# Channel attention and two gated layers: block 0 goes through the softmax itself, and the softmax is folded into w_in beside it

## The chip, the core and the metric

The kernel runs on one core of a Trainium2 chip. The metric is the time of one execution on the device, in microseconds (us). The kernel before took 1212.53 us (median of three runs, 1211.35 to 1214.38). The profile shown here was taken in a further execution of 1211.48 us.

## The reference

There are 6016 tokens of 256 channels. q, k, v and all weights come as 64-bit floating point numbers or 32-bit ones; the kernel computes in 32 bits.

```
qn = q / (norm over tokens of q + 1e-6);  kn likewise
a  = softmax(kn^T qn / tau)          # 256 x 256, over the last axis
x  = v @ a                           # 6016 x 256
h  = x @ w_in                        # 6016 x 2048
P  = a0 + a1 h + a2 h^2 + a3 h^3;    Q = 1 + |b0||h| + |b1| h^2
y  = (P / (Q + 1e-6)) @ w_out        # 6016 x 256
g  = sigmoid(y @ w_gate);  u = y @ w_val          # 6016 x 1536 each
out = (g * u) @ w_out2
```

## The kernel before, in words

**Two arithmetics.** A matmul of 32-bit floats (`f32`) takes four passes of the systolic array. Most of the kernel splits each operand instead into a rounded high part and the rest (`hi`, `lo`, type `fp32r`) and adds three one-pass products. A split costs a copy (on ACT or DVE) and a subtraction (on DVE or POOL).

**Stage 1, scores and norms.** q and k lie interleaved in `kqk` and are loaded in 15 chunks of one, two or four tiles of 128 tokens (`LOADS`). For each tile TensorE adds k^T q into `s_ps` (L488, f32): 256 columns for chunks marked `s` in `KG`, 384 for chunks marked `g`, whose extra columns give the squared norms of k on the diagonal. ACT squares each chunk (L509), DVE or POOL add some of the squares up (L518, `UNIT` says which), and TensorE sums them over the tokens (L457: all-ones weights by 256 columns, L461: squares as weights by one column of ones) into `nrm`. So the norms of q stand along the free axis, the same in all partitions, and those of k one to a partition.

**Loads.** All big loads go through SyncE's queue in the order of the string `ORDER` (`x` a chunk of `kqk`, `n` the tokens of v of block 0, `i`, `o`, `g`, `v`, `2` chunks of w_in, w_out, w_gate, w_val and w_out2, 1 MB each as 64-bit numbers). A chunk of `kqk` is put into the room of a weight that is loaded later. a, b and tau are loaded from ACT's queue at the start.

**Weights.** Each of the 17 weight chunks is turned into 32-bit floats: ACT scales the upper words (L679), ACT or DVE shifts the lower ones (L682 or L686, the string `TOP`), DVE joins the two (L690). Then it is split: high part on ACT or DVE (L807 or L811, `HI`), rest on DVE or POOL (L814, `LOW`).

**Softmax.** From `nrm` and the diagonals come 1/norm (L574 to L588; for q with DVE operations on 256 columns), then the scaled scores and their row maximum (L600), the exponentials with row sums (L608), the row sums' reciprocals (L621), the transposes of the exponentials (L615) and their copy to SBUF (`et_sb`, L625). `WARM` matmuls without a use (L632) may run while TensorE has nothing else.

**Fold.** v @ a @ w_in is computed as v @ (a @ w_in): each of the four chunks of w_in (512 columns) is multiplied by the transposed exponentials (L739, f32), and the evacuation from PSUM multiplies by the reciprocal row sums: L753/L756 for chunk 0, which is kept whole and split later by L774/L778, and L759/L761 for chunks 1 to 3, which are split at once.

**Blocks.** The tokens are then worked in 12 blocks, block 0 of 384 tokens and the rest of 512. A block's first layer has 8 steps: h of 256 columns of w_in (L899 in f32 for the two steps of block 0 that use chunk 0; L884/L886/L888 as three products otherwise, for which v is split by L849/L852), three ACT passes over h (L908 to L912), the rational function on DVE, ACT and POOL (L914 to L936; the reciprocal is a seed with an arctangent correction), and the sum into y (L946 in f32 for block 0, L964 to L974 later). The second layer of a block (L1010 to L1047) runs between the first-layer steps of the next.

**Order.** Every operation is given an engine, a cost and a due time; a planner in the kernel lays them out by these, and each engine's instructions are then issued in that order. The dictionaries `VT`, `VT0`, `VT1`, `WT` hold the due times and the strings above the choices of engine and buffer. An engine works its list strictly in order: an instruction that waits holds up all behind it.

Of the kernel before, what the change touches and what calls it, by code (L numbers as in the profile page):

```python
# [9 lines left out]
F32 = mybir.dt.float32  # L10
# [29 lines left out]
VT1 = {'h': -17955.3, 'u': 1533.3, 'ab': -991.9, 'sq': -3411.4, 'v': -162.2, 'w': 1751.0, 'Q': -2494.2, 'seed': 18354.6, 't': -325.8, 'at': -3730.8, 'y': 617.1, 'g': 2768.2, 'hi': 2217.8, 'lo': -1222.6, 'yh': 2990.1, 'yl': 344.8, 'G': 4863.1, 'sig': -6142.7, 'sv': -15292.6, 'hi2': 3414.6, 'lo2': 2277.0, 'oh': -11134.2, 'ol': -140.4, 'base': 851.8, 'ev': 2619.7}  # L40

VT0 = {'h': -1990.9, 'u': 14971.4, 'ab': -134.3, 'sq': 11037.5, 'v': 4305.9, 'w': -9165.5, 'Q': -4668.5, 'seed': 15588.7, 't': -6249.8, 'at': -10702.8, 'y': -4704.4, 'g': -1165.7, 'hi': 757.1, 'lo': -493.3, 'yh': 4573.9, 'yl': -5536.7}

WT = {'ci': -142.1, 'ci_d': -17724.1, 'co': 1739.6, 'co_d': 5275.5, 'cg': 1385.4, 'cg_d': 1785.4, 'cv': -1917.9, 'cv_d': -1783.3, 'c2': -4767.0, 'c2_d': 2905.7, 'wp': -3829.7, 'wp_d': 241.4, 'b0': 7059.9, 'b1': -3149.2, 'b2': -3.8, 'm0': -8935.8, 'm1': 3.6, 'e0': -6822.5, 'cvl': 2835.9, 'alt': 5000.0, 'wpp': 4734.9, 'v0': -3576.2, 'ri': -4427.7, 'ri_d': 11199.1, 'ro': 12944.7, 'ro_d': -9707.8, 'cvm': 4036.8}


ORDER = 'xxxxxxxinxxgogxxxxov2x2ix2oiogivv'
# [18 lines left out]
WARM = 8  # L66
# [46 lines left out]
class Plan:  # L113
# [40 lines left out]
    def schedule(self):  # L154
# [67 lines left out]
        while len(order) < len(self.ops):  # L222
# [54 lines left out]
def tile_channel_attention_two_moes(  # L277
# [78 lines left out]
    class Weight:  # L356
# [36 lines left out]
        def keys(self, col):  # L393
            return [(self.key(col), p, h) for p in range(2) for h in range(2)]
# [52 lines left out]
    def sum_mm(sq, n, q_only):  # L447
        first_sum["n"] = first_sum.get("n", 0) + 1

        def run():  # L450
            first_sum["n"] -= 1
            late = not first_sum["n"]
            w = C if q_only else 2 * C
            v_ = sq.ap().rearrange("p a c -> p (a c)")
            for i in range(n):
                q0 = i * w + (0 if q_only else P)
                mm(out=nrm.ap()[:, 0:C], lhsT=ones, rhs=v_[:, q0:q0 + C], start=0 not in first_sum,  # L457
                   stop=late and i == n - 1 and q_only)
                first_sum[0] = True
                for h in () if q_only else (0, 1):  # L460
                    mm(out=nrm.ap()[:, C + h:C + h + 1], lhsT=v_[:, i * w + 3 * P * h:i * w + 3 * P * h + P],  # L461
                       rhs=ones[:, 0:1], start=False, stop=late and i == n - 1 and h == 1)
        return run
# [30 lines left out]
    for k, (c, i, n) in enumerate(units):  # L494
# [18 lines left out]
        elif direct:  # L513
            pl.op(PE, n * (.433 if g else .893), t_s + (c + .7) * SUM_AT, sum_mm(sq, n, g), [sq, "ones"], [nrm], tail=0.01)
# [13 lines left out]
    for k, (x, lo_, n) in enumerate(((a, 0, 4), (b, 4, 2), (tau, 6, 1))):  # L528
        pl.op(ACT, .1, -30000.0 + k, lambda x=x, lo_=lo_, n=n: nc.scalar.dma_start(
            out=sm[:, lo_:lo_ + n], in_=bcast(x, n)), (), ["sm_" + "abt"[k]], tail=2.4)  # L530

    def coefs():
        V = nc.vector
        V.tensor_scalar(out=cf[:, 0:4], in0=sm[:, 0:4], scalar1=KAPPA, scalar2=None, op0=ALU.mult)
# [4 lines left out]
        V.tensor_scalar(out=cf[:, 6:7], in0=cf[:, 6:7], scalar1=4.0, scalar2=None, op0=ALU.mult)  # L539

# [9 lines left out]
    pl.op(DVE, 0.6, -29000.0, coefs, ["sm_a", "sm_b", "sm_t"], ["cf", "sm_c"], port=True)  # L550
# [5 lines left out]
    rn = pl.buf("w", [P, 3, C], at=t_n)  # L556

    def diag_k():
        for h in range(2):
            nc.vector.scalar_tensor_tensor(  # L560
                out=rn.ap()[:, 2, :P], in0=s_ps.ap()[:, h, h * C:h * C + P], scalar=1.0, in1=ident, op0=ALU.mult,
                op1=ALU.mult, accum_out=sm[:, 22 + h:23 + h])

    def nrm_add():
        nc.vector.tensor_tensor(out=sm[:, 22:24], in0=sm[:, 22:24], in1=nrm.ap()[:, C:C + 2], op=ALU.add)

    if any(kg):
# [6 lines left out]
    pl.op(ACT, c_act(C, 1, 1), tn, lambda: nc.scalar.activation(  # L574
        out=rn.ap()[:, 1, :], in_=nrm.ap()[:, 0:C], func=ACTF.Sqrt, bias=sm[:, 8:9]), [nrm, "sm_tiny"], [(rn, 1)])
    pl.op(ACT, .2, tn, lambda: nc.scalar.activation(
        out=cf[:, 14:16], in_=x2(), func=ACTF.Sqrt, bias=sm[:, 8:9]), [xk, "sm_tiny"], ["sm_n"])

    def twice_norm(x, root, y):
        V = nc.vector  # L580
        V.reciprocal(out=y, in_=root)
        V.tensor_tensor(out=y, in0=x, in1=y, op=ALU.mult)
# [539 lines left out]
```

## Time and profile before

| | |
|---|---|
| median of three runs | 1212.53 us |
| the profiled execution | 1211.48 us |
| its span, first to last instruction | 1209.4 us |
| TensorE (PE) busy | 1177.8 us, 97% |
| VectorE (DVE) busy | 974.2 us, 81% |
| ScalarE (ACT) busy | 834.6 us, 69% |
| GpSimd (POOL) busy | 521.2 us, 43% |
| data moved | 43.30 MB |

The shares are means over stages of different kinds. The span is best cut at about 62 us (norms complete), 81 us (first useful matmul after the softmax) and 150 us (all weights ready, blocks overlap). The profile's "granted clock" is the share of full speed that TensorE got in a stretch. A matmul of f32 leaves two rows in the trace, so a count of 16 stands for 8 matmuls.

### The profile page before, as it was taken

The page shows a single profiled execution, that of the slowest core. Times are in us where ns is not written, and L with a number is a line of the kernel's source. Part 1 is how long each engine was busy: PE and PEld are TensorE (multiplying, and loading weights), DVE is VectorE, ACT ScalarE, POOL GpSimd, SP SyncE. Part 2 cuts the span into 40 slices and gives each one's busy share as a digit, 9 for nine tenths or more (in the row PEclk, how much of TensorE's full clock was granted, in tenths as well). Part 3 has the DMA queues.
Part 4 walks back from the last instruction along what each step waited for, and adds up shares of the span by engine and source line. Part 5 has one row for each costly group of instructions (what it writes and reads, how often), then busy time and mean ns, then how long its engine had stood idle before and what let it go on. Part 6 is the DMA issues. An engine that isn't in the chain of part 4 may idle for free.

```text
span 1209.4 us, 13151 instructions
## 1 busy us (share of the span) xinstructions
PE 1177.8 (97%) x5160; PEld 963.6 (80%) x5160; DVE 974.2 (81%) x838; ACT 834.6 (69%) x983; POOL 521.2 (43%) x266
## 2 busy tenths in 40 slices
PE   7968999999999999999999999999999999999998
PEld 5845699788888888888888888888888888888877
DVE  2799988798788789788789789789888878878911
ACT  5778877676677677677677577677677677667622
POOL 5523255355354345345345345345345435435422
PEclk9979999999999999999999999999999999999999
DMA  9960000000100100100100100100000000000000
GB/s 361 400 251 18 18 1 1 31 1 1 36 1 1 35 1 1 35 1 1 35 1 1 35 1 1 36 1 1 29 7 1 18 18 1 18 1 1 18 1 17
DMA packets 15613, 43.30 MB, mean 36 GB/s; under 512 B 1344, under 2 KB 1856, under 8 KB 14272
## 3 DMA queue, kind: packets, MB, share of 16 engines
q1 hardware_dynamic: 14976, 42.21, 9.3%
q8 instruction: 40, 0.66, 0.2%
q10 hardware_dynamic: 576, 0.27, 0.1%
q14 instruction: 21, 0.17, 0.0%
HBM read 36.31 MB, written 6.16 MB: 35 GB/s over the span
## 4 chain that ended last, share of the span: by engine, by line
PE 87%; DVE 5%; DMA 4%; ACT 2%; issue 1%; POOL 0%; SPq 0%; DVEq 0%
PE pO L1039 10%; PE pH L884 6%; PE pH L886 6%; PE pH L888 6%; PE pY L974 6%; PE pY L966 6%; PE pY L964 6%; PE pG L1010 5%; PE pV L1010 5%; PE pG L1012 5%; PE pO L1047 5%; PE pV L1012 5%; PE pG L1014 5%; PE pV L1014 5%; DMA win<-in_kqk_dram 2%; DMA wo<-in_moe_w_out_dram 1%
## 5 line engine op out<-in xcount | busy, mean ns | idle before, releaser
L1032 POOL TENSOR_TENSOR lo<-sig,hi 128x512 fp32r<-128x512 f32 (+1 forms) x143 | 248.8, 1745 | 337.6 <-ACT hi L1028 337.6
L956 POOL TENSOR_TENSOR lo<-w,hi 128x1024 fp32r<-128x1024 f32 x88 | 217.1, 2467 | 265.3 <-ACT hi L951 218.4
L933 DVE SCALAR_TENSOR_TENSOR a<-a,s 128x1024 f32<-128x1024 f32 (+1 forms) x94 | 167.6, 1784 | 54.1 <-ACT a L930 54.1
L910 ACT ACTIVATE a<-pH,cf 128x1024 f32<-128x1024 f32 (+1 forms) x92 | 101.7, 1105 | 100.0 <-PE pH L888 100.0
L1039 PE MATMUL pO<-hi,wo 128*128 128x512 f32 (+1 forms) x580 | 151.6, 383 | 0.0
L920 DVE SCALAR_TENSOR_TENSOR a<-a,s 128x1024 f32<-128x1024 f32 (+1 forms) x94 | 113.6, 1209 | 46.7 <-ACT s L912 44.9
L884 PE MATMUL pH<-vhi,win 128*128 128x512 f32 (+1 forms) x364 | 141.8, 390 | 2.6 <-DVE w L917 2.6
L936 DVE SCALAR_TENSOR_TENSOR w<-w,cf,a 128x1024 f32<-128x1024 f32 (+1 forms) x95 | 140.2, 1476 | 2.9
L888 PE MATMUL pH<-vhi,win 128*128 128x512 f32 (+1 forms) x364 | 141.3, 388 | 0.0
L886 PE MATMUL pH<-vlo,win 128*128 128x512 f32 (+1 forms) x364 | 141.3, 388 | 0.0
L930 ACT ACTIVATE a<-a 128x1024 f32<-128x1024 f32 (+1 forms) x96 | 99.9, 1041 | 58.2 <-DVE a L928 56.3
L1025 DVE TENSOR_TENSOR sig<-sig,pV 128x512 f32<-128x512 f32 (+2 forms) x145 | 96.6, 667 | 53.0 <-PE pV L1014 51.9
L928 DVE TENSOR_TENSOR a<-a,s 128x1024 f32<-128x1024 f32 (+1 forms) x89 | 138.2, 1553 | 0.0
L964 PE MATMUL pY<-hi,wo 128*128 128x512 f32 x352 | 137.1, 390 | 0.0
L966 PE MATMUL pY<-hi,wo 128*128 128x512 f32 x352 | 137.1, 389 | 0.0
L1028 ACT ACTIVATE hi<-sig 128x512 fp32r<-128x512 f32 (+2 forms) x145 | 90.5, 625 | 58.0 <-DVE sig L1025 57.6
L1039 PEld LDWEIGHTS pO<-hi,wo 128*128 128x128 f32 x580 | 108.1, 188 | 21.0
L917 DVE SCALAR_TENSOR_TENSOR w<-w,cf,pH 128x1024 f32<-128x1024 f32 (+1 forms) x92 | 116.4, 1265 | 1.7
L1010 PE MATMUL pG<-yhi,wg 128*128 128x512 f32 (+1 forms) x288 | 112.2, 389 | 1.6 <-ACT yhi L985 1.1
L1023 ACT ACTIVATE sig<-pG 128x512 f32<-128x512 f32 (+2 forms) x145 | 85.3, 589 | 39.8 <-PE pG L1014 24.2
L1012 PE MATMUL pG<-ylo,wg 128*128 128x512 f32 (+1 forms) x288 | 111.0, 385 | 0.8 <-DVE ylo L987 0.8
L1010 PE MATMUL pV<-yhi,wv 128*128 128x512 f32 (+1 forms) x288 | 110.9, 385 | 0.0
(231 smaller groups left out, 2322.4 us busy)
## 6 DMA issues: line engine op xcount, KB each, us to landing
wo<-in_moe_w_out_dram SPq DMA_DIRECT2D x7, 1024.0 KB, 15.9
wo<-in_kqk_dram SPq DMA_DIRECT2D x6, 1024.0 KB, 13.6
v<-in_v_dram SPq DMA_DIRECT2D x11, 512.0 KB, 3.6
out_dram<-v SPq DMA_DIRECT2D x10, 512.0 KB, 2.8
win<-in_moe_w_in_dram SPq DMA_DIRECT2D x4, 1024.0 KB, 15.2
wg<-in_moe_w_gate_dram SPq DMA_DIRECT2D x3, 1024.0 KB, 19.0
wv<-in_moe_w_val_dram SPq DMA_DIRECT2D x3, 1024.0 KB, 16.5
win<-in_kqk_dram SPq DMA_DIRECT2D x2, 1024.0 KB, 16.5
```

What stands on the lines that cost most here:

```text
L884: mm(out=hp.ap()[:, i, :n], lhsT=WIN.at(f * P, 0, z), rhs=vhi.ap()[:, z, :n], start=(z == 0), stop=False)
L886: mm(out=hp.ap()[:, i, :n], lhsT=WIN.at(f * P, 0, z), rhs=vlo.ap()[:, z, :n], start=False, stop=False)
L888: mm(out=hp.ap()[:, i, :n], lhsT=WIN.at(f * P, 1, z), rhs=vhi.ap()[:, z, :n], start=False, stop=(z == 1))
L933: pl.op(DVE, c_dve(N), vt + vp['y'] * d, lambda: stt(out=V(y_), in0=V(a_), scalar=ATAN_C, in1=V(s_), op0=ALU.add, op1=ALU.mult), [a_] + S_ ...
L936: pl.op(DVE, c_dve(N, 1), vt + vp['g'] * d, lambda: stt(out=V(w_), in0=V(w_), scalar=col(A0), in1=V(y_), op0=ALU.add, op1=ALU.mult), [w_, ...
L956: lambda: e_lo.tensor_tensor(out=V(lo), in0=V(w_), in1=V(hi).bitcast(F32), op=ALU.subtract),
L964: mm(out=y_ps.ap()[:, z, :n], lhsT=WO.at(f * C, 0)[:, sl], rhs=hi.ap()[:, i, :n], start=(f == 0), stop=False)
L966: mm(out=y_ps.ap()[:, z, :n], lhsT=WO.at(f * C, 1)[:, sl], rhs=hi.ap()[:, i, :n], start=False, stop=False)
L1010: mm(out=gp[i].ap()[:, :n], lhsT=wt.at(f * P, 0, z), rhs=yhi.ap()[:, z, :n], start=(z == 0), stop=False)
L1012: mm(out=gp[i].ap()[:, :n], lhsT=wt.at(f * P, 0, z), rhs=ylo.ap()[:, z, :n], start=False, stop=False)
L1032: lambda sg=sg, hi=hi, lo=lo, sl=sl, e=e: e.tensor_tensor(out=lo.ap()[:, sl], in0=sg.ap()[:, sl], in1=hi.ap()[:, sl].bitcast(F32), op=ALU. ...
L1039: mm(out=o_ps.ap()[:, z, sl], lhsT=WO2.at(f * C, i)[:, z * P:(z + 1) * P], rhs=hi.ap()[:, sl], start=(f == 0 and i == 0), stop=False)
```

## The change

- **Block 0.** The exponentials are divided by their row sums in place (`over`, on DVE, per half). v of block 0 is multiplied by them on TensorE (`x_mm`, four f32 matmuls of 384 columns), ACT copies the result to SBUF (`x0`), and all eight steps of block 0 multiply x0 by w_in as it is (f32, `h_plain`). v of block 0 is no longer split.
- **Fold.** The transposes and the fold of w_in come with later due times, for use from block 1 on. Every half chunk of 256 columns is folded by itself into the PSUM tile pG or pV, and goes from there to its split parts at once: high part on ACT, rest on DVE. L753 to L778 go.
- **Norms.** The squares of q too are summed with the squares as weights and one column of ones: four columns of `nrm` in place of 258. 1/norm is four DVE operations on 128 x 4; those of q are put on a diagonal (`diag_q`), spread over the partitions by two matmuls with all-ones weights, and copied to SBUF.
- **Small loads.** a, b and tau go through SyncE's queue, b and tau after the fifth load, a after the 25th.
- **Replanned.** ORDER, KG, UNIT, PLC (which room a chunk of `kqk` takes), TOP, HI, LOW, the buffers, and all due times of blocks 0 and 1 and of the weights are new; those of the later blocks are not. WARM is 6 in place of 8.

```diff
-ORDER = 'xxxxxxxinxxgogxxxxov2x2ix2oiogivv'
+ORDER = 'xx2xvxxxgxvxxxxxgxxoxoiioiongvi22'
-KG = 'ssgsssssssssgss'
+KG = 'ggssssssssssgsg'
-TOP = 'aaaddaaaaadddddda'
-HI = 'dadaaaddaddad'
-LOW = 'ddddpppppddpp'
-T_PS = '...YYHHYYY.Y2YYHY'
+TOP = 'adaaaaaddaaddadad'
+HI = 'dadadaadddaaa'
+LOW = 'pdppdpdpppppp'
+T_PS = 'HYYYH..HYY.YYYY..'
-S0 = 'gssssssg'
-T0 = 'pppppdpd'
+S0 = 'sssgsgsg'
+T0 = 'pdpdpppd'
...
-                mm(out=nrm.ap()[:, 0:C], lhsT=ones, rhs=v_[:, q0:q0 + C], start=0 not in first_sum,
-                   stop=late and i == n - 1 and q_only)
...
+                for m, c0 in ((0, 0), (1, P)) if q_only else ((2, 0), (0, P), (1, 2 * P), (3, 3 * P)):
+                    mm(out=nrm.ap()[:, m:m + 1], lhsT=v_[:, i * w + c0:i * w + c0 + P], rhs=ones[:, 0:1],
...
+        def over(h=h):
+            r = sm[:, 18 + h:19 + h]
+            nc.vector.tensor_scalar(out=r, in0=sm[:, 16 + h:17 + h], scalar1=1e-9, scalar2=None, op0=ALU.add)
+            nc.vector.reciprocal(out=r, in_=r)
+            nc.vector.tensor_scalar(out=e_sb.ap()[:, h, :], in0=e_sb.ap()[:, h, :], scalar1=r, scalar2=None,
+                                    op0=ALU.mult)
...
+            for z in range(2):
+                mm(out=x_ps.ap()[:, z, :n0], lhsT=e_sb.ap()[:, h, z * P:(z + 1) * P], rhs=nat0.ap()[:, h, :n0],
+                   start=h == 0, stop=h == 1)
...
+            pl.op(ACT, c_act(2 * m, 1), pv, lambda part=part, both_=both_: nc.scalar.activation(
+                out=part(0), in_=both_(), func=ACTF.Copy), [two], [(key, 0, q)])
+            pl.op(DVE, c_dve(2 * m), pv, lambda part=part, both_=both_: nc.vector.tensor_tensor(
+                out=part(1), in0=both_(), in1=part(0).bitcast(F32), op=ALU.subtract), [two, (key, 0, q)], [(key, 1, q)])
...
+            def h_plain(i=i, f=f):
+                w = win_f[f // 4][0]()
+                for z in range(2):
+                    mm(out=hp.ap()[:, i, :n], lhsT=w[:, z, f % 4 * P:f % 4 * P + P], rhs=nat.ap()[:, z, :n],
+                       start=(z == 0), stop=(z == 1))
```

## Rows read from the trace of the kernel before

**Rows 1.** The page's first part: busy time, share of the span, instructions of each engine.

```profile
PE 1177.8 (97%) x5160; PEld 963.6 (80%) x5160; DVE 974.2 (81%) x838; ACT 834.6 (69%) x983; POOL 521.2 (43%) x266
```

**Rows 2.** Windows: stretch, length, busy time of each engine, granted clock, DMA share, GB/s.

```profile
0.00:62.65 62.65, 55.08 (x238) 44.69 (x238) 31.98 (x35) 42.31 (x44) 33.44 (x22) 1.00 0.97 381
62.65:80.84 18.19, 6.81 (x22) 5.55 (x22) 17.81 (x33) 12.08 (x17) 4.72 (x2) 0.62 0.95 370
80.84:150.00 69.16, 63.23 (x235) 42.21 (x233) 66.03 (x73) 56.98 (x71) 19.20 (x12) 1.00 0.05 16
150.00:1204.00 1054.00, 1051.75 (x4664) 870.43 (x4663) 857.72 (x699) 722.66 (x851) 463.84 (x231) 1.00 0.03 11
50.00:139.60 89.60, 71.51 (x275) 50.04 (x274) 86.62 (x107) 70.65 (x89) 28.22 (x16) 0.92 0.38 142
```

**Rows 3.** Timeline of PE in stage 1: start, length, instruction, count, idle before.

```profile
14.05 5.32 PE L488 MATMUL pO<-wo 128*128 128x384 f32 x16
33.02 7.07 PE L488 MATMUL pO<-wo 128*128 128x256 f32 x32
53.57 1.13 PE L488 MATMUL pO<-wv 128*128 128x256 f32 x4 [1.39 <-DMA wv<-in_kqk_dram]
55.33 0.68 PE L457 MATMUL gv<-w,ones 128*128 128x256 f32 x2
56.21 1.97 PE L457 MATMUL gv<-w,ones 128*128 128x256 f32 x8
```

**Rows 4.** Timeline of all engines from 62 to 81 us, norms to fold.

```profile
62.63 2.36 POOL L814 TENSOR_TENSOR wo<-s,wo 128x1024 fp32r<-128x1024 f32 x1 [3.98 <-DVE wo L811]
63.77 2.30 DVE L690 SCALAR_TENSOR_TENSOR lo<-lo,win 128x1024 int32<-128x1024 int32 x1
68.30 0.31 ACT L576 ACTIVATE cf<-sm 128x2 f32<-128x2 f32 x1
69.53 1.74 DVE L581 RECIPROCAL w<-w 128x256 f32<-128x256 f32 x1
72.22 1.75 DVE L584 RECIPROCAL w<-w 128x256 f32<-128x256 f32 x1
74.03 4.63 PE L632 MATMUL gv<-w,ones 128*128 128x256 f32 x10 [11.38 <-DVE w L584]
75.35 0.16 DVE L583 SCALAR_TENSOR_TENSOR cf<-cf 128x2 f32<-128x2 f32 x1
76.49 0.48 DVE L600 CUSTOM_DVE_ANT_0 a<-pO,w,sm 128x256 f32<-128x256 f32 x1
78.46 1.06 PE L615 MATMUL pH<-ident,a 128*128 128x128 f32 x4
80.84 1.89 PE L739 MATMUL pH<-w,s 128*128 128x256 f32 x8
```

**Rows 5.** Timeline of PE and DVE late in block 0.

```profile
116.10 0.33 PE L884 MATMUL pO<-vhi,win 128*128 128x384 f32 x1
118.01 0.33 PE L888 MATMUL pO<-vhi,win 128*128 128x384 f32 x1
118.18 5.32 PE L946 MATMUL pY<-w,yhi 128*128 128x384 f32 x16
138.58 1.02 DVE L936 SCALAR_TENSOR_TENSOR w<-w,cf,a 128x768 f32<-128x768 f32 x1
```

**Rows 6.** Windows of 50 to 139.6 us for DVE's lines L686, L690, L811, L814, in turn.

```profile
50.00:139.60 89.60, 7.77 (x7) 0.92 0.38 142
50.00:139.60 89.60, 16.87 (x13) 0.92 0.38 142
50.00:139.60 89.60, 5.18 (x6) 0.92 0.38 142
50.00:139.60 89.60, 7.30 (x6) 0.92 0.38 142
```

**Rows 7.** The same window for ACT's line L682.

```profile
50.00:139.60 89.60, 5.78 (x5) 0.92 0.38 142
```

More of the change, by code (lines that the diff above doesn't have):

```diff
@@ L455, in run @@
             for i in range(n):
-                q0 = i * w + (0 if q_only else P)
-                mm(out=nrm.ap()[:, 0:C], lhsT=ones, rhs=v_[:, q0:q0 + C], start=0 not in first_sum,
-                   stop=late and i == n - 1 and q_only)
[L459 to L462, printed above, removed]
+                for m, c0 in ((0, 0), (1, P)) if q_only else ((2, 0), (0, P), (1, 2 * P), (3, 3 * P)):
+                    mm(out=nrm.ap()[:, m:m + 1], lhsT=v_[:, i * w + c0:i * w + c0 + P], rhs=ones[:, 0:1],
+                       start=0 not in first_sum, stop=late and i == n - 1 and m == (1 if q_only else 3))
+                    first_sum[0] = True
         return run
@@ L478, in tile_channel_attention_two_moes @@
         place = spare[max(0, len(spare) - (nch - c))] if spare else min(later, key=lambda w: used[w])
+        if PLC[c] >= 0:
+            place = later[PLC[c] % len(later)]
         used[place] = c
@@ L574, in tile_channel_attention_two_moes @@
[L574 to L580, printed above, removed]
+        pl.op(DVE, 2 * c_dve(P) + .1, tn, diag_k, [s_ps, "ident", "sm_tiny"], [(rn, 3), "sm_k2"])
+    pl.op(DVE, .2, tn, lambda: nc.vector.tensor_tensor(out=x4, in0=x4, in1=nrm.ap()[:, 0:4], op=ALU.add),
+          [nrm, "sm_k2", "sm_tiny"], ["sm_x"])
@@ new lines, in tile_channel_attention_two_moes @@
+    pl.op(DVE, .8, tn, over_norm, ["sm_x", "sm_n"], ["sm_y"], port=True)
+    qn = pl.buf("pG", [P, 512], at=t_n)
+    for h in range(2):
+        pl.op(DVE, .25, tn, lambda h=h: diag_q(h), ["sm_y", "cf", "ident"], [(rn, h)], port=True)
+        pl.op(PE, c_pe(P, 4), tn, lambda h=h: mm(out=qn.ap()[:, h * P:(h + 1) * P], lhsT=ones, rhs=rn.ap()[:, h, :P],
+                                                 start=True, stop=True), [(rn, h), "ones"], [qn])
+    pl.op(DVE, c_dve(C) + .05, tn, lambda: nc.vector.tensor_copy(rn.ap()[:, 2, :], qn.ap()[:, 0:C]), [qn], [(rn, 2)])
@@ L614, in e_tr @@
+    for z in range(2):
+        if X0_EV[z] == "a":
+            pl.op(ACT, c_act(n0, 1), tn + 6, lambda z=z: nc.scalar.activation(
+                out=x0.ap()[:, z, :n0], in_=x_ps.ap()[:, z, :n0], func=ACTF.Copy), [(x_ps, z)], [(x0, z)])
+        else:
+            pl.op(DVE, c_dve(n0), tn + 6, lambda z=z: nc.vector.tensor_copy(
+                x0.ap()[:, z, :n0], x_ps.ap()[:, z, :n0]), [(x_ps, z)], [(x0, z)])
+    def e_tr():
+        for h in range(2):
             for j in range(2):
-                nc.tensor.transpose(out=et_ps.ap()[:, 0, j * C + h * P:j * C + (h + 1) * P],
+                nc.tensor.transpose(out=et_v()[:, j * C + h * P:j * C + (h + 1) * P],
@@ L838, in load_v @@
         vt = start[b_] - 6.0 if b_ else WT['v0']
-        nat = pl.buf("v", [P, 2, NB], at=start[b_] - 1.0 if b_ else -190.0)
+        if not b_:
+            return x0, None, None
+        nat = pl.buf("v", [P, 2, NB], at=start[b_] - 1.0)
         N = n * P
-        dma(vt - 10 if b_ else turn("n", 0), lambda: nat.ap()[:, :, :N], vv[:, :, t0 * P:t0 * P + N],
-            n * C * 4 * P, (), [(nat, 0), (nat, 1)])
-        if b_ == 0 and all(x == "r" for x in HR):
-            return nat, None, None
+        dma(vt - 10, lambda: nat.ap()[:, :, :N], vv[:, :, t0 * P:t0 * P + N], n * C * 4 * P, (), [(nat, 0), (nat, 1)])
         hi, lo = (pl.buf(t_, [P, 2, NB], F32R, at=start[b_]) for t_ in ("vhi", "vlo"))
```

240 lines of the change are left out of this document (97 added, 143 removed).

## The prediction, made before the changed kernel ran

> **What bounds the kernel now.** I read the page's busy shares first, then windows, then the timelines of the stages that the windows set apart. TensorE is busy 97% of the span and VectorE 81% [rows 1], but the windows show two regimes [rows 2]. From 150 to 1204 us PE is busy 1051.75 of 1054 us at full clock: nothing is to be had there except less PE work, and the change leaves those blocks alone. Ahead of 150 us PE idles 7.6 us before 62.65 (the wait for the first data, and 1.39 us for the last chunks of k and q [rows 3]), 11.4 us between 62.65 and 80.84, and 5.9 us from there to 150. The second stretch is the worst one: PE has nothing from the last norm sum to the end of the second 256-wide reciprocal, then runs matmuls without a use at a granted clock of 0.62 on average (a mix of the levels 1.2 and 2.4 GHz), and the first folding matmul starts at 80.84 [rows 4]. Of 18.19 us only the transposes (1.06) are useful, so 17.1 us are lost. In the same time, and on to the last operation of block 0 on DVE at 139.6 [rows 5], DVE is busy 86.62 of 89.6 us [rows 2]. So this stage has two bounds, the chain of the softmax as PE sees it, and DVE as a resource; ACT follows with 70.65 us.
>
> **Part by part.** The sums are made against the profiled execution, 1211.48 us (span 1209.4 and 2.1 around it); the median is 1.05 us above it, and I add that at the end.
>
> *Norm sums.* A tile with 256 squares of q and two columns for k takes 0.88 us (55.33 to 56.21), the 256 columns alone 1.97/4 = 0.49 [rows 3]; so two single columns cost about 0.4, four about 0.8. Before, 7 tiles of the short form and 6 of the long make 7 x 0.49 + 6 x 0.88 = 8.7 us; after, 6 x 0.4 + 5 x 0.8 = 6.4. One tile fewer runs at 384 columns (5.32/4 = 1.33 against 7.07/8 = 0.88 [rows 3]): -0.45. The last chunk of k and q has 6 MB of weights ahead of it in the order in place of 9 MB and v0; at 381 GB/s [rows 2] 18.6 MB are through at 49 us, so PE no longer waits for it: -1.39. Together -4.1. Bounds: zero, if a chunk waits for the room that an earlier one still holds (the eighth, tenth, eleventh and fourteenth take a room for the second time), and -4.1. Nearest to the rows is most of it: I take -2.7, norms complete at 60.0.
>
> *Softmax.* Out go the two reciprocals of 256 columns (1.74, 1.75) and two operations between them. In come an addition and four operations on 128 x 4 (0.16 each, 0.2 apart), a square root on ACT (0.31), two diagonals, two matmuls (about 0.5), a copy of 256 columns (at most 0.48) [rows 4]. With handoffs: addition 0.4, root 0.4, 0.8, diagonals 0.6, matmuls 0.75, copy 0.6, two scores 1.3, second exponential 0.6, its division 0.75: 6.2 us (an estimate from these rows), so 66.2. Upper bound: as long as before, 62.65 to 78.46, 15.8. v0 comes after 12 weight chunks and all of k and q, 25.3 MB; 23.9 are through at 62.65, the rest at 370 GB/s takes 3.9 us [rows 2]: 66.5. Both land together; x0's matmuls start at 66.5, and late is whichever slips. The wait of 6.5 us lets the clock fall again; I charge 2.5 us for matmuls at the low level.
>
> *Work that PE gains.* x0: 4 matmuls of 384 columns at 5.32/8 = 0.665 [rows 5] = 2.7 us, on the path. h of block 0: 32 such matmuls = 21.3, against 8 of them and 72 one-pass ones at (118.01 - 116.10)/11 = 0.174 [rows 5] = 17.8: +3.5. The fold's columns are the same. PE alone then gives -2.7 (norms), -8.1 (17.1 lost become 6.5 + 2.5), -5.9 (the stalls after 80.84), +6.2: **-10.5**, if nothing else holds it up.
>
> *DVE, the term that decides.* From 50 us on the weights cost it 7.77 + 16.87 + 5.18 + 7.30 = 37.1 us [rows 6]. After, 13 chunks are left at 50 us (w_out2's first, two of w_val, one of w_gate come earlier): 13 joins at 1.22 (7.30/6 [rows 6] for the same 1024 columns) = 15.9, 3 shifts 2.1, copies 2.6, 4 subtractions 4.9: 25.5, so -11.6. The softmax falls from about 7.6 to 5.7 (its rows counted up as above): -1.9; folding from 5.5 to 5.0 (eight subtractions of 512 columns at half of 1.22 + 0.01): -0.5; one more step of block 0 multiplies on DVE instead of POOL (T0, S0): +0.95. Against that, 37.1 holds some 4 us in which DVE stood beside POOL: the join at 63.77 took 2.30 in place of 1.22 while a POOL subtraction ran from 62.63 to 64.99 [rows 4]. I expect 3 of these again, since POOL gets six subtractions of weights where it had four: +3. Sum -10.0; DVE's rows overlap by some 5% (each starts before the last one's end), so **-9.5**. DVE idled 3.0 of 89.6 us [rows 2]. In the new chain it waits for ACT's root, for the two spreading matmuls and the exponentials, and five weight chunks land only after 66 us: idle between 3 and 13 us more than before is 0 in the best case; I take 3.5 more, nearest to the row. That makes **-6.0**.
>
> The Trainium skill (SBUF — State Buffer, section "SBUF: two separate sides") says that an operation of VectorE with two SBUF inputs and one of GpSimd that reads SBUF exclude each other for a whole instruction. By that rule each subtraction of 2.36 us moved to POOL can hold DVE back by up to its own length, 14 us for six; the trace agrees in kind, with 1.08 us lost at 63.77.
>
> *ACT.* It loses the splits of v0 and the scaling of the fold, and gains the shifts: five before (5.78/5 = 1.16 each [rows 7]), ten now: +5.8, two more high parts +2.1, one more upper word +1.1, less about 1.5 elsewhere: +7.5, on 70.65 of 89.6 [rows 2]. In a stage 6 us shorter that is 78 of 83.6. It hides, but only just; if not, it costs up to 7.5.
>
> *Edits at nothing.* The small loads take three issues from ACT's queue, idle then, to SyncE's, where loads run ahead of their data; b, tau and a are needed only after 60 us, and DVE has gaps before 50 (31.98 busy of 62.65 [rows 2]). If a comes late it stops DVE's list for as long as it is late. Splits of w_out and w_out2 that are left at the end of block 0 fall into blocks where ACT and DVE have room (DVE 857.72 of 1054 [rows 2]).
>
> **Rivals.**
> *PE packs (B).* DVE's surplus idle does not come and PE's stalls vanish: -10.5, so 1201 to 1202. For it: all three engines start block 0 earlier, and h no longer waits for the fold. Against: DVE was 97% busy there and stays near that.
> *The gain is given back (C).* POOL's subtractions fall beside block 0's two-input DVE operations, six at 1.08 = 6.5 us, and the -6.0 become about zero: 1212 to 1213. For: POOL at 62.63 shows it. Against: the kernel's planner books such operations apart, and POOL's total in the stage stays near 28 us [rows 2].
> *It doesn't do what it says (E).* The fold's due times lie ahead of block 0's, so if the weights are ready first, PE folds for up to 15 us (8 x 1.89 [rows 4]) before h starts, while x0 and h in f32 still cost 6.2: about 1213. Against: w_in's last chunk lands after v0.
> *ACT becomes the bound (D), the slower side.* The place is the weights' shifts and high parts between 50 and 140 us. ACT's 19 us of idle there were waits for others; if they stay, its 78 us of work end 7.5 us later than before and PE pays for x0 as well: -6 turns into +6, 1218 to 1219. It decides from the point at which ACT idles more than about 11 us in the stage; slower by a measurable amount from 15.
>
> **How the numbers follow.** Forecast 1211.48 - 6.0 + 1.05 = **1206.5**, with 1203 to 1210 its own range: 0.50; B 0.15, C 0.17, E 0.06, D 0.12. 0.3%, about what a measurement can tell from no change, is 3.6 us: faster below 1208.9, slower above 1216.2. Faster: 0.43 of the forecast's 0.50, and B: 0.58. Same: 0.07 of the forecast, 0.14 of C, 0.05 of E: 0.26. Slower: D and 0.04 of C and E: 0.16. Low end 1199 (B with v0 and the norms on time, and no cold matmuls, 2.5 less), high end 1216 (D's start).
>
> **What would show it.** Norms complete near 60 and the last k and q not waited for; x0's matmuls near 66.5, with either v0 or the second division as the last thing before; h of block 0 from about 70, mixed with folding; block 0's last DVE operation at 133 to 134 in place of 139.6; DVE's weight lines after 50 us near 26 us plus waits; ACT near 78 us in the stage. The steady blocks should not move. I am wrong if x0 starts after 75 (no gain) or 79 (slower), if ACT is what DVE and PE wait for, or if PE idles more than 6 us in all between x0 and the end of block 0.

## The result, and the profile after

The changed kernel takes 1221.88 us (median of four runs, 1221.58 to 1223.01) where the kernel before took 1211.94 beside it: a ratio of 1.0081, with a 95% interval of 1.0063 to 1.0098. It is slower by about 10 us; the forecast was 1206.5, in a range of 1199 to 1216. The profiled execution took 1221.94 us, with a span of 1220.1.

Page of the changed kernel, first part, as in [rows 1]:

```profile
PE 1186.0 (97%) x5182; PEld 967.6 (79%) x5182; DVE 965.0 (79%) x841; ACT 837.8 (69%) x984; POOL 510.2 (42%) x261
```

DVE and POOL have less to do, PE 8 us more, and still the whole is longer. Windows of the changed kernel, columns as in [rows 2]:

```profile
0.00:62.65 62.65, 52.16 (x242) 42.59 (x242) 36.24 (x42) 40.59 (x43) 27.30 (x20) 1.00 0.94 363
62.65:80.84 18.19, 12.19 (x43) 9.03 (x43) 12.59 (x30) 14.15 (x19) 2.00 (x1) 0.62 0.98 372
80.84:150.00 69.16, 61.41 (x209) 38.41 (x208) 60.90 (x67) 54.48 (x69) 19.45 (x10) 1.00 0.09 31
300.00:350.00 50.00, 47.71 (x203) 38.58 (x202) 38.84 (x33) 33.97 (x40) 19.29 (x10) 0.97 0.07 22
50.00:139.60 89.60, 75.85 (x286) 51.43 (x285) 73.94 (x98) 73.22 (x90) 23.88 (x12) 0.92 0.39 145
```

The last line holds the surprise. DVE is busy 73.94 us there against 86.62 [rows 2], so DVE idles 15.7 us where it idled 3.0, and ACT idles 16.4. Nobody is the bound there, so somebody waits. In part DVE has less to do, as forecast, and in part block 0 is not yet done: its last DVE operation ends at 145.0 us instead of 139.6. Up to there DVE is busy 79.3 of 95.0 us, and idles 15.7 again (the last line of block 0 on DVE, and the window up to its end):

```profile
143.97 1.02 DVE L919 SCALAR_TENSOR_TENSOR w<-w,cf,gv 128x768 f32<-128x768 f32 x1
50.00:145.03 95.03, 80.66 (x303) 54.71 (x302) 79.30 (x104) 77.42 (x95) 24.19 (x12) 0.93 0.38 142
```

The fourth line of the windows above (300 to 350 us) is a second surprise: PE was to be busy throughout the steady blocks, and misses 2.29 us there, part of the rest at a lower clock. Half of the loss (5.3 us) is there when the second layer of block 0 starts (PE, before and after); the other half comes later.

```profile
146.17 0.33 PE L1010 MATMUL pG<-yhi,wg 128*128 128x384 f32 x1
151.51 0.33 PE L993 MATMUL pG<-yhi,wg 128*128 128x384 f32 x1
```

Three places show where. First, stage 1 (timeline of PE, the lines with an idle time, as in [rows 3]):

```profile
20.39 3.72 PE L489 MATMUL pO<-wg 128*128 128x256 f32 x16 [3.24 <-DMA wg<-in_kqk_dram]
31.75 3.72 PE L489 MATMUL pO<-win 128*128 128x256 f32 x16 [0.74 <-DMA win<-in_kqk_dram]
36.79 3.72 PE L489 MATMUL pO<-win 128*128 128x256 f32 x16 [1.31 <-DMA win<-in_kqk_dram]
56.73 1.13 PE L489 MATMUL pO<-win 128*128 128x256 f32 x4 [0.78 <-DMA win<-in_kqk_dram]
```

PE waits 6.1 us for kqk, and the last sums end at 64.5. Then the softmax and the fold (timeline of all engines, changed kernel, answering to [rows 4]):

```profile
66.51 0.17 DVE L542 TENSOR_SCALAR cf<-sm 128x4 f32<-128x4 f32 x1 [1.81 <-DMA sm<-in_moe_a_dram]
67.20 0.15 DVE L571 TENSOR_TENSOR sm<-sm,gv 128x4 f32<-128x4 f32 x1
69.74 1.22 PE L591 MATMUL gv<-w,ones 128*128 128x128 f32 x4 [5.25 <-DVE w L584]
70.76 1.06 PE L663 MATMUL gv<-w,ones 128*128 128x256 f32 x2
71.86 0.42 DVE L593 COPY w<-gv 128x256 f32<-128x256 f32 x1 [1.91 <-PE gv L663]
77.67 2.85 PE L635 MATMUL pH<-v,a 128*128 128x384 f32 x8 [0.24 <-DVE hi L721]
80.35 1.89 PE L754 MATMUL gv<-hi,v 128*128 128x256 f32 x8
82.08 1.89 PE L754 MATMUL gv<-vhi,v 128*128 128x256 f32 x8
84.01 0.60 ACT L766 ACTIVATE win<-gv 128x512 fp32r<-128x512 f32 x1 [1.46 <-PE gv L754]
84.64 0.69 DVE L768 TENSOR_TENSOR win<-gv,win 128x512 fp32r<-128x512 f32 x1 [1.24 <-ACT win L766]
86.16 1.99 PE L754 MATMUL gv<-hi,v 128*128 128x256 f32 x8 [0.90 <-ACT win L766]
89.74 1.99 PE L754 MATMUL gv<-vhi,v 128*128 128x256 f32 x8 [0.29 <-ACT win L766]
```

Two things are to be seen. The addition of the norms (L571) stands on DVE behind a small operation that waits 1.81 us for `a`. And everything in pG and pV carries one name, `gv`: the copy L593 reads what L591 wrote into pG, and yet waits for L663, a matmul without a use into pV. The fold at 82.08 goes into the other bank than the one at 80.35; nevertheless the first eviction (84.01) waits until the second fold has ended, and the third fold (86.16) waits for evictions of the other bank.

The third place is the end of block 2 (timeline of PE, ACT and DVE):

```profile
319.40 0.61 PE L1030 MATMUL pO<-lo,wo 128*128 128x512 f32 x2
319.82 1.28 DVE L919 SCALAR_TENSOR_TENSOR w<-w,cf,a 128x1024 f32<-128x1024 f32 x1
321.20 1.06 ACT L934 ACTIVATE hi<-w 128x1024 fp32r<-128x1024 f32 x1
322.31 0.52 PE L947 MATMUL pY<-hi,wo 128*128 128x512 f32 x1 [2.29 <-ACT hi L934]
323.06 0.63 PE L947 MATMUL pY<-hi,wo 128*128 128x512 f32 x1
```

PE has done all it had (the second layer of block 1, and block 2's y up to its seventh step) when the eighth step still goes through DVE and ACT. It idles 2.29 us, and the next matmuls come 0.43 us apart instead of 0.23: from 322.3 to 326.7 the granted clock is 0.61, mostly the lower level, 1.2 GHz. Before, the y of block 2's last two steps followed the second layer there, and PE had no gap.

### The profile page after: what moved, and what is told of

Read it like the earlier page. It is cut to its first block, busy times and chain, and to the rows that moved or that the text cites. A ratio compares the mean times of both kernels' runs of the same rounds, so it can differ in the third digit from the quotient of the medians.

```text
span 1220.1 us, 13195 instructions
## 1 busy us (share of the span) xinstructions
PE 1186.0 (97%) x5182; PEld 967.6 (79%) x5182; DVE 965.0 (79%) x841; ACT 837.8 (69%) x984; POOL 510.2 (42%) x261
## 4 chain that ended last, share of the span: by engine, by line
PE 89%; DVE 5%; DMA 4%; ACT 1%; issue 1%; SPq 0%; DVEq 0%; ACTq 0%
PE pO L1022 10%; PE pY L949 7%; PE pY L947 7%; PE pH L872 6%; PE pH L874 6%; PE pH L876 6%; PE pY L957 6%; PE pG L993 5%; PE pV L993 5%; PE pG L995 5%; PE pV L995 5%; PE pV L997 5%; PE pG L997 5%; PE pO L1030 5%; DMA win<-in_kqk_dram 2%; PE pO L489 1%
## 5 line engine op out<-in xcount | busy, mean ns | idle before, releaser
L916 DVE SCALAR_TENSOR_TENSOR a<-a,s 128x1024 f32<-128x1024 f32 (+1 forms) x93 | 162.4, 1748 | 57.5 <-ACT a L913 57.5
L903 DVE SCALAR_TENSOR_TENSOR a<-a,s 128x1024 f32<-128x1024 f32 (+1 forms) x93 | 112.7, 1212 | 49.7 <-ACT s L895 48.1
L872 PE MATMUL pH<-vhi,win 128*128 128x512 f32 x352 | 137.3, 390 | 0.8 <-DVE w L900 0.8
L874 PE MATMUL pH<-vlo,win 128*128 128x512 f32 x352 | 137.1, 390 | 0.0
L876 PE MATMUL pH<-vhi,win 128*128 128x512 f32 x352 | 137.1, 389 | 0.0
L993 PE MATMUL pG<-yhi,wg 128*128 128x512 f32 (+1 forms) x288 | 112.1, 389 | 1.6 <-ACT yhi L968 1.1
L993 PE MATMUL pV<-yhi,wv 128*128 128x512 f32 (+1 forms) x288 | 111.6, 388 | 0.0
## 6 DMA issues: line engine op xcount, KB each, us to landing
wo<-in_moe_w_out_dram SPq DMA_DIRECT2D x7, 1024.0 KB, 13.2
```

What stands on the lines that cost most here:

```text
L872: mm(out=hp.ap()[:, i, :n], lhsT=WIN.at(f * P, 0, z), rhs=vhi.ap()[:, z, :n], start=(z == 0), stop=False)
L874: mm(out=hp.ap()[:, i, :n], lhsT=WIN.at(f * P, 0, z), rhs=vlo.ap()[:, z, :n], start=False, stop=False)
L876: mm(out=hp.ap()[:, i, :n], lhsT=WIN.at(f * P, 1, z), rhs=vhi.ap()[:, z, :n], start=False, stop=(z == 1))
L916: pl.op(DVE, c_dve(N), vt + vp['y'] * d, lambda: stt(out=V(y_), in0=V(a_), scalar=ATAN_C, in1=V(s_), op0=ALU.add, op1=ALU.mult), [a_] + S_ ...
L993: mm(out=gp[i].ap()[:, :n], lhsT=wt.at(f * P, 0, z), rhs=yhi.ap()[:, z, :n], start=(z == 0), stop=False)
```

## The experiments

Each ratio is to the kernel before, run beside it; 0.001 is 1.2 us. An interval is some 0.001 to either side, so a difference of two runs is known to about 2 us. The changed kernel itself had 1.0081, and 1.0087 in a repeat (e5). The expectations were written with other words for the layers: their "first square" and "second square" are a block's first and second layer (in the first of them "block 0's first square" is the Square pass of one of its steps), and a gate matmul is L993, the first of the second layer.

**e1: separate tiles.** In the changed kernel pG and pV are one tile of two banks until block 0 is done, though only three steps of block 0 (the Square pass of their h) use both banks at once. Here they are tiles of their own until the first such step.

```diff
-            if self.pool is None:
-                return gv[:, "GV".index(self.tag[1]), :]
             return self.pool.tile(shape, dtype, tag=tag, name=name)
...
+    for tag in ("pG", "pV"):
+        pools[tag].pool = two_own.enter_context(tc.tile_pool(name="r0_" + tag, bufs=1, space=PSUM))
+    def join_gv():
+        if not gvs:
+            two_own.close()
...
```

> The changed kernel with one thing undone: the two PSUM banks pG and pV are tiles of their own while the softmax and the fold use them, and become one shared tile only when block 0's first square needs both. Order, plan and arithmetic are untouched. Theory H2 (the shared tile makes each fold, each eviction and the softmax's spread copy wait for work in the other bank): the copy L593 no longer waits 1.91 us for a warm matmul, block 0's matmuls with x0 start at about 76.5 instead of 77.67, DVE's 15.7 us of idle time in 50 to 139.6 falls by 3 us or more, and the whole takes 2 to 4 us less, 1218 to 1220. Rival (DVE's and POOL's hold on each other, or ACT's load, sets block 0's pace, and these waits lie inside longer ones): within 0.5 us of the changed kernel, 1221.4 to 1222.4.

Measured: 1213.39 us, ratio 1.0014 (1.0005 to 1.0023). That is 0.0073 or 8.8 us less than the repeated changed kernel, more than twice what I had expected (2 to 4). Windows of this kernel, the second from x0's first matmul to the first gate matmul of block 0's second layer:

```profile
50.00:139.60 89.60, 80.32 (x311) 55.56 (x309) 81.21 (x106) 77.62 (x95) 23.64 (x11) 0.94 0.41 153
76.00:142.99 66.99, 64.53 (x225) 42.20 (x225) 63.57 (x70) 58.47 (x72) 21.27 (x10) 1.00 0.16 57
```

In the changed kernel that second stretch is 73.84 us (77.67 to 151.51). The order is the same and the work is the same; DVE's idle time between 50 and 139.6 fell from 15.7 to 8.4 us. The shared tile is shown as the main cause.

The gap at the end of block 2 is there in e1 too, but in the profiled execution no half clock follows it (two lines of PE's timeline; the matmuls after them come 0.23 us apart):

```profile
314.22 0.50 PE L954 MATMUL pY<-hi,wo 128*128 128x512 f32 x1 [2.29 <-ACT hi L941]
314.56 0.39 PE L956 MATMUL pY<-hi,wo 128*128 128x512 f32 x1
```

So the gap does not bring the half clock each time, and this profile, of an execution of 1211.31 us, lies 2.1 us below e1's median; how often it is so is not known.

**e2: small loads.** a, b and tau are issued by `nc.scalar` in place of `nc.sync`, ahead of everything (`early` holds the three).

```diff
-        for o in pl.schedule():
+        plan = pl.schedule()
+        for o in early + [x for x in plan if x not in early]:
             o.fn()
```

> The changed kernel with the three small loads a, b and tau issued from ACT's queue ahead of everything, as the kernel before had its small loads away from SP's queue; all else in the planned order. Theory H1 (three loads of 128 small pieces each stand in the queue that brings kqk and the weights, so the stream of kqk falters at 13 to 17 us and PE idles 3.24 us at 20.39, and a lands at 66.4, 1.81 us after DVE could use it): PE's idle of 3.24 us goes, the norm sums are complete at 61.0 to 61.5 instead of 64.4, the wait for a goes, x0's matmuls start 3 to 4.5 us earlier, and the whole takes 3 to 4 us less, 1218 to 1219. Rival (kqk's stream is set by the order of the weight loads in it, and the later stalls at 31.75, 36.79 and 56.73 grow by what the first one gives back): norms at 64 still, only the 1.8 us of a's wait can go, 1220 to 1222.

Measured: 1219.83, ratio 1.0069 (1.0055 to 1.0083): 2.2 us less by ratio than the repeat, between the theory and the rival, and by itself hardly clear of the noise. x0 starts at 74.00 in its trace, 3.7 us earlier, but block 0 takes 73.9 us as before and the gap at block 2's end stays.

**e3: steady order.** The operations of blocks 1 and on and of all second layers are emitted in the order of the kernel before.

```diff
+        for i, x in zip(places_, STEADY):
+            plan[i] = by[n0_ + x]
```

> The changed kernel with the operations of blocks 1 and on, and of every second square, issued in the order that the kernel before has for them; they hold the same places among the operations of stage 1 and block 0, whose order is untouched. The two orders differ only in blocks 1 and 2 and the second squares of blocks 0 and 1. Theory H4 (the new plan let the second square of block 1 run out before block 2's last first-square step, so that PE idles 2.29 us at 322 and then works at half clock until 326.7): that gap and the half clock go, PE is busy 50.0 of 50 in 300 to 350, and the whole takes about 4 us less, 1217.5 to 1218.5. Rival (the gap is a late DVE or ACT chain that follows from block 0's lateness whatever the order): the gap stays or another of its size opens in blocks 1 or 2, 1221 to 1223.

Measured: 1216.98, ratio 1.0048 (1.0035 to 1.0060), 4.7 us less than the repeat of the changed kernel. The window at block 2's end:

```profile
300.00:350.00 50.00, 49.99 (x220) 40.73 (x219) 38.64 (x32) 33.43 (x40) 21.76 (x12) 1.00 0.07 22
```

**e4: all three.**

> The three edits together: separate tiles for pG and pV in the fold, small loads on ACT's queue, the order of before for blocks 1 and on. If the three theories hold and their gains lie at different times, they add: 9 to 11 us less than the changed kernel, 1211 to 1213, no better than before but no worse. If block 0's pace has another cause (DVE and POOL, ACT, or the fold going ahead of block 0's h), only the 4 us of the steady order and what the norms gain arrive: 1215 to 1217.

Measured: 1206.81, ratio 0.9958 (0.9946 to 0.9970). The single gains (8.8, 2.2, 4.7) make 15.7 us, the three together 15.6: they add. (Against the first measurement of the changed kernel, 1.0081, the single gains make 13.6 us and the three together 14.9; the sum holds within the noise by either.) Expected was no better than before; it is faster, because e1 gave more. Windows of this kernel, the last one up to the end of block 0 on DVE:

```profile
50.00:139.60 89.60, 81.97 (x312) 56.88 (x312) 82.47 (x108) 78.17 (x96) 23.73 (x11) 0.94 0.38 144
73.19:140.16 66.97, 64.50 (x225) 42.20 (x226) 63.57 (x70) 58.02 (x72) 21.36 (x10) 1.00 0.16 55
50.00:133.60 83.60, 76.14 (x292) 53.20 (x292) 76.77 (x103) 74.50 (x93) 23.73 (x11) 0.94 0.41 154
```

**e5: the changed kernel again.**

> The changed kernel itself, beside the three that follow. All theories: 1220 to 1222, and PE's stall at about 20 us between 1.3 and 3.7 us (it was 3.24, 3.68 and 1.35 in three profiles with the same order of loads).

Measured: 1221.59, ratio 1.0087 (1.0073 to 1.0100); PE's stall at 20 us was 3.06.

**e6: e4 without its small loads.**

> Separate tiles and the steady order, but a, b and tau left in SP's queue: the version with all three edits less the small loads. Theory H1 (the small loads cost what the sum of the first four runs leaves for them once the folds no longer hide it: 14.0 less 7.4 less 3.8): 2.8 us above the version with all three, 1209 to 1210. Rival (their cost is the 1.0 us that moving them was worth alone, and the rest of the sum is chance): 1207.5 to 1208.2.

Measured: 1209.15, ratio 0.9982 (0.9973 to 0.9990). The small loads cost 0.0024 or 2.9 us in this company. x0 starts at 77.56 against 73.19, and the second layer at 144.52 against 140.16: in the traces the whole delay of 4.4 us goes through block 0. (The times differ by less; e4's profile has a granted clock of 0.67 from 1150 to 1155 us, which is worth 1.7 us, and e6's has full clock in that place.)

**e7: e4, but only `a` leaves SP's queue.**

> The version with all three edits, but only a is issued from ACT's queue; b and tau stay in SP's queue at their planned places. If b and tau, which stand ahead of kqk's pieces and hold the stream at 13 to 17 us, are the costly ones: the PE stall at 20 us is back (1.3 to 3.7 us), DVE waits some 6 us for b and tau at its start, and the time is 1.5 to 3 us above the version with all three, 1208.3 to 1209.8. If a's lateness at 66 us is the costly one: within 0.5 us of it, 1206.3 to 1207.3.

Measured: 1206.07, ratio 0.9958 (0.9946 to 0.9970), as e4. By my own wording that put the cost on `a`'s lateness, but the trace said otherwise: the stall at 20 us was gone too, with b and tau where they had been. Windows of 2 us in the changed kernel, then in e7 (last column GB/s):

```profile
2.00:4.00 2.00, 0.00 (x0) 0.00 (x0) 0.00 (x0) 0.01 (x1) 0.00 (x0) 1.00 0.93 317
12.00:14.00 2.00, 2.00 (x14) 1.68 (x13) 0.00 (x0) 2.00 (x3) 1.55 (x1) 1.00 0.82 226
14.00:16.00 2.00, 2.00 (x11) 1.77 (x10) 0.00 (x0) 1.54 (x2) 0.81 (x1) 1.00 0.37 140
```

```profile
2.00:4.00 2.00, 0.00 (x0) 0.00 (x0) 0.00 (x0) 0.46 (x1) 0.00 (x0) 1.00 0.60 171
4.00:6.00 2.00, 0.00 (x0) 0.00 (x0) 0.00 (x0) 0.00 (x0) 0.00 (x0) 1.00 0.60 179
12.00:14.00 2.00, 2.00 (x12) 1.61 (x11) 0.98 (x1) 0.98 (x2) 0.00 (x0) 1.00 0.99 397
```

The stream is slow for about 4 us in either; only the place differs. Why b and tau in SP's queue make no second dip here is open.

**e8: own tiles for the softmax alone,** shared from the first fold on, with the other two edits of e4.

```diff
             def w_mm(sbv=sbv, psv=psv, q=q, m=m):
+                join_gv()
...
```

> The version with all three edits, but pG and pV are tiles of their own only until the first fold; from there on the folds use the halves of the shared tile, as in the changed kernel. If the price of the shared tile is the fold's chain (a fold into one bank waits for the evictions of the other): block 0, from its matmuls with x0 to the first gate matmul of the second square, takes 73 to 74 us again instead of 67, and the time is 1213 to 1214. If it is the softmax's copy alone: 67 us, and 1206.5 to 1207.5.

Measured: 1214.02, ratio 1.0022 (1.0014 to 1.0031), 7.8 us above e4, and from x0 to the second layer:

```profile
73.86:147.75 73.89, 66.11 (x224) 41.71 (x225) 63.83 (x70) 58.41 (x71) 21.43 (x10) 1.00 0.14 47
```

73.9 us again. The price is the fold's chain, eight folds that wait for each other's evictions; the copy in the softmax is the small part.

**e9: e4, but `a` stays in SP's queue** and only b and tau leave it.

> The version with all three edits, but b and tau alone are issued from ACT's queue at the start and a stays in SP's queue at 58 us. The run with a alone moved was as fast as the one with all three moved, so the two costs of a late a and of a faltering stream can be told apart here. If the stream falters at 12 to 16 us only where no small load has gone first (183 GB/s there against 383 to 420): it does not falter here, a's wait of 1.3 to 1.8 us is the only loss left, and the time is 1207 to 1208. If a's place in the queue is the whole cost: 1209 to 1210, as with all three small loads in SP's queue.

Measured: 1206.72, ratio 0.9961 (0.9948 to 0.9974). There is no dip at 12 to 16 us (399 and 430 GB/s); DVE waits 1.33 us for `a`, x0 starts 0.8 us later than in e7, and the time is that of e4 within the interval. So the late `a` costs nothing that the times can tell (in the traces the second layer starts 0.8 us after e7's, at 141.39), though it makes a dip of its own: 222 GB/s at 60 to 62 us. The dip at 12 to 16 us costs about 3 us more than the slow start that takes its place, and each of the three choices of what to send first from ACT's queue (`a`, b and tau, all three) made that exchange.

**e10: the mirror of e3,** the kernel before with the new order of blocks 1 and on.

> The kernel before with the operations of blocks 1 and on and of every second square issued in the changed kernel's order, at the places that these hold; the mirror of the run with the steady order. Theory H4 (the order alone makes the gap at the end of block 2): a gap of about 2.3 us and half clock for some 4 us appear near 317 us, and the time is 1214.5 to 1215.5. Rival (the order only costs where block 0 is late): 1211 to 1212.

Measured: ratio 1.0029 (1.0017 to 1.0042), 3.5 us, and the gap is there to the hundredth (window, and the line of PE's timeline after it):

```profile
295.00:345.00 50.00, 47.70 (x203) 38.61 (x202) 38.35 (x33) 33.80 (x40) 19.91 (x10) 0.97 0.07 22
```

```profile
315.72 0.64 PE L1094 MATMUL pY<-hi,wo 128*128 128x512 f32 x1 [2.29 <-ACT hi L1081]
```

The order alone does it, also where block 0 is not late.

**e11: a short softmax.** e7 with the chain ahead of the weights' work on DVE and ACT, and x0's PSUM in pO: norm sum, root, 1/norm, diagonals (89 to 94) and x0's evictions (107, 108) go ahead of weight work, weight work (140, 170, 171) behind scores, exponentials and divisions.

```diff
+                    x_ps.t = pools["pO"].tile([P, 2, 512], F32, tag="pO", name="pO")
...
+        for n, at_, after in ((89, 128, 0), (90, 128, 0), (91, 130, 0), (92, 130, 0), (94, 130, 0), (140, 99, 1),
+                              (170, 102, 1), (171, 103, 1), (106, 105, 1), (107, 204, 0), (108, 204, 0)):
+            plan.remove(by[n])
+            plan.insert(plan.index(by[at_]) + after, by[n])
```

> The version with all three edits (a alone on ACT's queue), with the softmax chain put ahead of the weight work that stands in its way on DVE and ACT: norm addition and root ahead of win's conversions, the two conversions and a shift of DVE behind the diagonals, the scores and the divisions, one ACT conversion behind the exps, the evictions of x0 ahead of two ACT conversions, and x0's matmuls write the pO room instead of pH, so that they don't wait for a conversion there. The prediction had 6.2 us from the norms to x0's matmuls; this tests how much of the 10 us measured is the queue and what it is worth. If the pace of block 0 is PE's, x0 starts at 70.5 to 71.5 instead of 73.6 and the time is 1203.5 to 1205. If DVE's list sets it (the same conversions only come later): x0 earlier, but the time within 0.7 us of 1206.1.

Measured: 1207.18, ratio 0.9962 (0.9949 to 0.9975), no gain over e7. x0 starts at 70.41, 3.2 us earlier, and PE gives most of it back (lines of PE, ACT and DVE):

```profile
70.41 2.75 PE L778 MATMUL pO<-v,a 128*128 128x384 f32 x8
71.05 1.17 ACT L853 ACTIVATE s<-wg 128x1024 f32<-128x1024 f32 x1 [1.55 <-DMA wg<-in_moe_w_gate_dram]
77.03 1.23 DVE L864 SCALAR_TENSOR_TENSOR pY<-pY,wv 128x1024 int32<-128x1024 int32 x1 [2.45 <-ACT wv L856]
80.17 1.99 PE L897 MATMUL pV<-hi,v 128*128 128x256 f32 x8 [2.27 <-DVE win L911]
```

The second layer starts at 139.88 against 140.64 in e7. PE's fold waits for an eviction that stands in DVE's list behind a join of w_val, and this join starts at 77.03, as in e7 (77.07): it waits for ACT, which had waited for the load of w_gate. So what keeps the time here is DVE's list, as the prediction said of the stage, but by its order behind a late weight, while DVE itself idles 2.45 us, and not by how much it has to do.

**e12: e11 with a, b and tau as one piece each,** in one partition, spread by a matmul with ones. All three go first from ACT's queue, where e11 had `a` alone; e4 and e7 differ in just that, and take the same time.

```diff
-            out=sm[:, lo_:lo_ + n], in_=bcast(x, n))
+            out=row[0:1, lo_:lo_ + n], in_=x.rearrange("(o n) -> o n", o=1))
...
+        mm(out=t[:, 0:7], lhsT=ones[0:1, :], rhs=row[0:1, 0:7], start=True, stop=True)
+        nc.vector.tensor_copy(sm[:, 0:7], t[:, 0:7])
```

> The kernel with the short softmax chain, and a, b and tau each loaded as one piece into one partition from ACT's queue and spread over the partitions by one matmul with ones and one DVE copy. If the 128 small pieces of each such load slow the stream (170 to 230 GB/s at 2 to 6 us where they go first, against 310 without): PE's first matmul stands at about 4.2 us instead of 6.1 to 6.5, no dip follows at 12 to 16 us, the norms come 1.5 to 2 us earlier and the time is 1.5 to 2 us below the run before. If the slow start has another cause: the same time within 0.5 us.

Measured: 1204.76, ratio 0.9943 (0.9929 to 0.9957), 0.0019 or 2.3 us below e11; each of its five executions is faster than each of e11's five. The early windows of this kernel:

```profile
2.00:4.00 2.00, 0.00 (x0) 0.00 (x0) 0.00 (x0) 1.14 (x1) 0.00 (x0) 1.00 0.84 293
4.00:6.00 2.00, 1.34 (x2) 0.84 (x3) 0.00 (x0) 0.75 (x2) 0.00 (x0) 1.00 0.99 360
12.00:14.00 2.00, 2.00 (x8) 0.93 (x6) 0.00 (x0) 2.00 (x3) 1.24 (x1) 1.00 1.06 442
```

PE's first matmul stands at 4.66 us instead of 6.51, and no dip follows. But the norm addition on DVE (62.08) comes no earlier than in e11 (62.08), x0 starts at 70.79, and the second layer at 139.40, only 0.5 us before e11's. Much of the rest of the difference between the two profiles is at the start of the second layer of the last block (windows of e11, then e12):

```profile
1150.00:1155.00 5.00, 5.00 (x16) 3.95 (x15) 0.69 (x1) 0.98 (x2) 0.00 (x0) 0.66 0.00 0
1150.00:1155.00 5.00, 5.00 (x24) 4.13 (x23) 1.12 (x2) 1.82 (x3) 1.29 (x1) 1.00 0.00 0
```

After the same short wait of PE (1.88 us), e11's profiled execution ran at a granted clock of 0.66 there and e12's at full clock; 0.34 of 5 us is 1.7 us. Of the profiles that have it at full clock e7's has the slow start too. So of the 2.3 us, 0.5 are seen to come from the loads; whether the rest does is not shown.

This is the fastest version, 0.57% faster than before; e4, e7, e9 and e11 are 0.4% faster.

## Why the prediction was wrong, step by step

**The step that failed first** is the sentence on DVE's idle time: "I take 3.5 more, nearest to the row". It was 12.7 more (15.7 against 3.0 [rows 2]), while DVE's busy time up to the end of block 0 was 79.3 us against the 77.1 that the sum implies. I listed the root, the spreading matmuls, the exponentials and late chunks as what DVE would wait for, and of the fold only that its columns are the same. Its new path, eight half chunks through pG and pV with two evictions each, was never followed through the tile that both share. The rows had the name: the norm sums [rows 3] and the warm matmuls [rows 4] write `gv`. With separate tiles and the other two edits the step holds: in e4 block 0's last DVE operation ends at 133.6 ("133 to 134"), where the changed kernel has 145.0, and up to there DVE is busy 76.8 us and idles 6.8 (forecast 6.5).

The rule of the Trainium skill that bears on this (PSUM — Partial Sum Buffer, section "PSUM bank collisions raise a hardware error") is to guard PSUM by bank, or bank and quadrant. The rule is given there against collisions. Here the guard was a tile of two banks, which keeps the rule and more; what the more cost is shown by e1, with a guard for each bank: 8.8 us.

**"Edits at nothing": the small loads.** Mis-sized: 2.9 us (e6 against e4). I looked for a late `a`, which came true (1.81 us) and cost nothing that the times can tell (e9). The cost was the dip they make in the stream that stage 1 lives on.

The Trainium skill (DMA: Bandwidth & Descriptors, section "Bandwidth") calls transfers under 64 KB dominated by descriptors. These are of 0.5 to 2 KB in 128 pieces, and took 8 to 14 us from issue to landing in the changed kernel. The early windows of e12, with the same bytes in one piece each, agree with it: 293 and 360 GB/s against e11's 166 and 195.

**"The steady blocks should not move."** They did, by 4.7 us (e3) or 3.5 (e10). The due times of the later blocks were unchanged, yet the order that the planner made of them was not, and in the new order nothing covers block 2's last step. That the planner did so because block 0 leaves each engine at another time is my reading of it, and not tested. These three terms, 8.8 us, 2.2 (e2) and 4.7, are 15.7 us; the changed kernel is 15.4 above the forecast.

**Norms at 60.0, x0 at 66.5.** Both too early. The norms came at 64.5, and at 62.0 in the fastest version (e12). I had taken 1.39 us off because PE would not wait for the last chunk; it waited 6.1 us in all for kqk, 0.78 of them near the end. The softmax took 6.2 us only on paper: 13.2 from the end of the sums to x0 (64.5 to 77.67), 10.0 in e7 from the addition on (63.65 to 73.62), 8.3 in e11 (62.08 to 70.41). A shorter softmax alone was worth little: in e11 3.2 us of x0 are worth 0.8 at the second layer. Where the stream of loads is late, and with it the weights, the delay counts in full (e6: 4.4 us at x0 and at the second layer). "PE alone", -10.5, was not the bound.

**What held.** DVE's weight lines after 50 us make 27.4 us (2.08, 17.91, 2.60 and 4.78 for shifts, joins, copies and subtractions), forecast "near 26 us plus waits". The joins' surplus is one join that took 3.43 us in place of 1.22, at 55.74, beside a subtraction on POOL (55.72 to 58.09): 2.2 of the 3 us that I had set aside for such meetings. ACT was to be near 78 in the shortened stage: 74.5 in e4 up to 133.6, 77.4 in the changed kernel up to 145.0. "If PE idles more than 6 us in all between x0 and the end of block 0" was the right alarm: 7.75 us (73.84 - 66.09, from x0 to the second layer), and 2.5 in e1. That the forecast, 1206.5, is met by e4's 1206.81 is partly luck: x0 came 6.7 us later than assumed, and the stretch after it was shorter.

**The rivals.** E's picture was there (two folds ahead of the first h, at 83.81), but e1 keeps that order and loses the delay. D's sign was there too, ACT idling 16.4 us, past its point of 15; yet ACT worked more in e1 (77.62) and the time fell, so its idling was an effect. C is out: DVE's busy time fell by 7.3 us up to the end of block 0 (86.6 to 79.3; 9.9 in e4), near the 9.5 of the forecast, and of the joins only one met a subtraction on POOL. None of them named a false wait.

## What to carry to other kernels

When work moves into a buffer, ask by what unit its waits are kept: two banks in one tile make one queue of what could be two, and no busy share shows it; look for a wait whose releaser touches other data. A new plan moves what it does not touch: compare the order of the later blocks too, and put an order back to find its price. Count a small load by its pieces, not its bytes.

## What the runs showed that was not expected

- Three loads of 2.0, 1.0 and 0.5 KB, each as 128 pieces, hold the stream at 144 to 186 GB/s between 12 and 16 us when all three are in SP's queue (the changed kernel, e1, e3, e5, e6), where the kernels that send all three or b and tau first have 415 to 428. Sent first, they, or `a` alone, hold it at 175 to 199 between 2 and 6 us, where it has 312 to 327 without; in one piece each they leave it 293 and 360 there. The version with one piece each is 2.3 us faster (e12), of which 0.5 are traced to the loads.
- One gap of 2.29 us on PE, then 4.4 us at a granted clock of 0.61, cost 3.5 to 4.7 us together (e3, e10). In e1's profiled execution the same gap was followed by full clock.
- In stage 1 the same order of loads gave PE stalls of 3.24, 3.68, 1.35 and 3.06 us at about 20 us (the changed kernel, e1, e3, e5).
